# Attention bursts joined, cut with strips of several ordinary products, and TensorE's program aligned at six places, in a four-layer kernel on one core

## The chip, the core and the metric

The kernel runs on one of the eight cores of a Trainium2 chip. The metric is the time of one execution on the device in microseconds (us); lower is better. The core has engines that run side by side, each through its own list of instructions in order: TensorE (PE in the profile; its weight loads are PEld), VectorE (DVE), ScalarE (ACT), GpSimd (POOL) and SyncE (SP), which here issues nearly all DMAs. They wait for each other through semaphores.

## The reference

One sequence of 2048 positions with 448 features goes through two pairs of layers with the same weights in both pairs. Layer A is attention over 8 earlier positions at a distance of 2 (0, 2, ..., 14 back), with 16 heads of 28 features; layer B is a gated product.

```
def _A_ref(x, wqkv, wo):
    qkv = x @ wqkv                        # split in q, k, v; 16 heads of 28
    idx = pos[:, None] - (jnp.arange(8) * 2)[None, :]
    logits = einsum("bhsd,bhswd->bhsw", q, k[idx]) * 28 ** -0.5
    logits = where(idx >= 0, logits, -1e9)
    o = einsum("bhsw,bhswd->bhsd", softmax(logits), v[idx])
    return o.reshape(B, S, D) @ wo
def _B_ref(x, w_gate, w_up, w_down):
    return ((x @ w_gate) * (x @ w_up)) @ w_down      # 448 -> 1792 -> 448

x = x + _A_ref(layernorm(x), wqkv, wo)
x = x + _B_ref(layernorm(x), w_gate, w_up, w_down)
x = x + _A_ref(layernorm(x), wqkv, wo)
x = x + _B_ref(layernorm(x), w_gate, w_up, w_down)
```

## The kernel before

The layers are numbered 0 to 3 (A, B, A, B). The sequence is cut into chunks of 256 or 512 positions, and the chunks of the four layers are interleaved, so that layer 1 starts on the first chunk while layer 0 still works on later ones. `x_sb` holds the whole sequence on chip, all weights are loaded once.

**Ordinary products.** A product that sums over 448 features is cut into pieces of 64 rows. Two of them, on the two halves of TensorE's rows, run beside each other: the function `pair` makes one such step of two matmuls (recorded under L351). A unit is, for example, one block of 128 of the 1792 columns of layer B (`WGU`, 7 steps, 14 matmuls into two banks of PSUM), a pair of blocks of the down projection (`WD`), of the output projection (`wo_g`), of q and k (`WQK`) or of v (`WV`). `pair` also makes a second form of each step: 8 strips, each with 32 of the 128 columns of weights, on a tile of 64 x 32 of the array (L354). Eight strips do what the step's two matmuls do. A step whose end is signalled to another engine has no such form, and at most `MAXALT` = 6 steps of a unit have.

**Attention products.** Positions are worked on in blocks of 120 (the first of 128), two blocks a group, nine groups a layer. Here a group is named by layer and last block: S(0,10) is the scores of blocks 9 and 10 in layer 0. The scores "S" (L826) are keys times queries, in 64 small matmuls on tiles of 64 x 32; the groups named in `WIDE_S` take 32 matmuls on tiles of 64 x 64 in their place. ScalarE takes the exponential (L835), VectorE masks it with a minimum (L842). Then come 64 small matmuls "AV" (L860), the weighted sum of v together with the sum of weights, whose result is copied to `O_sb` (L871, L875), divided (L885 to L898) and goes into `oT`, the input of the output projection.

**Bursts.** The attention products use the array in another tiling than the ordinary ones, so they are issued as bursts. In the order of TensorE an entry `540*3.5/338` means: operation 540 (64 small products) is cut after 3 x 8 and 5 x 8 of them, at each cut one step of operation 338 is issued as its 8 strips, and what is left of 338 follows whole. An entry without `*` runs its small products one behind the other.

**What sets the order.** Nothing is decided at run time. `ORDER` has one string for each engine with the numbers of all operations in order; `BANKS` says which PSUM banks each operation of TensorE takes; both were written down by a search beforehand. `Sched.schedule` reads them, works out for each bank which operation must have released it, and `Sched.emit` issues the instructions with the waits on semaphores.

**Evictions.** Results leave PSUM by ScalarE or VectorE: q and k (`qk`, L701), v (`v_sb`, L766 to L793), gate by ScalarE to `g_sb` (L951), gate times up by VectorE to `hT` (L954), residuals by VectorE (L915). Layer norms take VectorE (L571, L573, L592) and ScalarE (L574, L576). The normed input is transposed by DMA (`dma_start_transpose`, SP) or, in layer 0, by TensorE (L602, L606).

Of the kernel before, what the change touches and what calls it, by code (L numbers as in the profile page):

```python
# [29 lines left out]
WIDE_S = ((0, 0), (0, 1), (0, 2), (0, 3), (0, 4), (0, 5))  # L30
MAXALT = 6
S_ORDER = (0, 4, 2, 6, 1, 5, 3, 7)
# [63 lines left out]
def grp_nc(g):  # L96
# [21 lines left out]
    ),  # L118
    "act": (
# [12 lines left out]
    ),  # L132
    "dve": (
# [18 lines left out]
    ),  # L152
    "pool": (
        "18 19 38 20 21 22 23 24 25 26 27 28 29 30 31 32 33 34 35 36 37"
# [45 lines left out]
class Sched:  # L200
# [22 lines left out]
    def schedule(self):  # L223
# [9 lines left out]
        for e in self.ENGS:  # L233
            self.order[e] = []
            for w in ORDER[e].split():
# [4 lines left out]
                if k:  # L240
                    short, cut, host = seq, [8 * int(c) for c in k.split(".")], self.ops[int(host)]
                    got.append(host)
                    k = len(cut)
                    cut += [len(short)]
                    seq, a = [], 0
                    for i, z in enumerate(cut):
                        seq += short[a:z]
                        a = z
                        if i < k:
                            seq += [(host, host.alt[i][q]) for q in (S_ORDER if short[z - 1][0].acquire.n == 4 else range(8))]  # L250
# [846 lines left out]
```

## Time and profile before

| | |
|---|---|
| median of 3 runs | 383.46 us (383.4, 383.46, 385.77) |
| profiled execution, first to last instruction | 380.8 us (the page gives no other time for it) |
| instructions profiled | 14251 |
| granted TensorE clock | 1.000 |
| DMA | 22.50 MB, mean 59 GB/s |

The profile is of one execution. It gives each engine's busy time, the chain of work that ended last, groups of instructions, waits with who ended them, and an order of time in which equal instructions are merged: start, length, engine, line, operation, output and inputs, shape, count. Matmuls are pipelined and their ends are modelled, so it is the starts of groups that tell how densely they follow. Shapes of matmuls are rows*columns of weights, then rows x moving columns.

### The profile page before, as it was taken

What the parts mean: (1) busy time and instruction counts of PE and PEld (TensorE: products, weight loads), DVE (VectorE), ACT (ScalarE), POOL (GpSimd) and SP (SyncE); (2) the same over time, 40 slices, a digit from 0 to 9 for tenths busy, and PEclk for the clock granted to TensorE, in tenths of its full rate; (3) what the DMA queues carried; (4) which work ended last, traced back from release to release, by engine and by line L of the source; (5) the groups of instructions that cost most, each with busy time, mean ns of one, the idle gap of its engine ahead of it and who ended that gap; (6) DMA issues with size and microseconds to landing.
All of it is one profiled execution on the core that took longest, in us unless ns stands there. A gap on an engine that the chain in (4) does not pass through costs nothing.

```text
span 380.8 us, 14251 instructions
## 1 busy us (share of the span) xinstructions
PE 375.8 (99%) x6322; PEld 210.2 (55%) x6322; DVE 287.0 (75%) x644; ACT 203.6 (53%) x389; POOL 5.1 (1%) x25
## 2 busy tenths in 40 slices
PE   8999999999999999999999999999999999999997
PEld 4645587545445445444756765545555444446664
DVE  8988999999976786787677985637998598455323
ACT  5997987746426652564465525547744635133320
POOL 5000000000000000000000000000000000000000
DMA  8656533600611034031101125320125004140002
GB/s 263 163 148 177 106 94 95 80 19 3 99 29 33 2 65 58 16 67 26 32 14 34 20 43 101 39 45 4 28 34 74 3 2 78 23 120 26 3 2 98
DMA packets 54881, 22.50 MB, mean 59 GB/s; under 512 B 45012, under 2 KB 54820, under 8 KB 54820
## 3 DMA queue, kind: packets, MB, share of 16 engines
q1 hardware_dynamic: 54676, 21.53, 27.6%
q8 instruction: 50, 0.82, 0.9%
q14 instruction: 11, 0.09, 0.1%
q10 hardware_dynamic: 144, 0.06, 0.1%
HBM read 8.54 MB, written 2.71 MB: 30 GB/s over the span
## 4 chain that ended last, share of the span: by engine, by line
PE 94%; DVE 2%; ACT 1%; issue 1%; DMA 1%; SPq 0%; DVEq 0%
PE ps L351 85%; PE ps L354 3%; PE ps L860 2%; PE ps L826 2%; PE ps L966 1%; ACT E_sb L835 1%; DMA x_sb<-in_A_x_dram 1%; DVE xn_sb L592 1%; DVE st L571 0%; PE ps L606 0%; DVE Qz L812 0%; DVE R_sb L885 0%; DVE E_sb L842 0%; SPq L443 0%; DVE qk L701 0%
## 5 line engine op out<-in xcount | busy, mean ns | idle before, releaser
L351 PE MATMUL ps<-xnTb,WGU 64*128 64x512 bf16 (+1 forms) x1894 | 172.4, 332 | 0.0
L351 PEld LDWEIGHTS ps<-xnTb,WGU 64*128 64x128 bf16 x1894 | 92.0, 94 | 69.8 <-issue 1.4
L951 ACT ACTIVATE g_sb<-ps 128x512 bf16<-128x512 f32 (+1 forms) x140 | 70.1, 510 | 85.0 <-PE ps L351 65.5
L954 DVE TENSOR_TENSOR hT<-g_sb,ps 128x512 bf16<-128x512 bf16 (+1 forms) x140 | 78.2, 575 | 46.9 <-ACT g_sb L951 44.4
L351 PE MATMUL ps<-WD,hT 64*128 64x448 bf16 x812 | 82.8, 350 | 0.0
L351 PEld LDWEIGHTS ps<-WD,hT 64*128 64x128 bf16 x812 | 38.9, 94 | 34.7 <-DVE hT L954 0.3
L351 PE MATMUL ps<-xnTa,WQK 64*128 64x512 bf16 (+1 forms) x494 | 53.0, 353 | 0.5 <-DVE WQK L518 0.3
L915 DVE TENSOR_TENSOR x_sb<-x_sb,ps 128x448 bf16<-128x448 bf16 x62 | 37.2, 614 | 14.7 <-PE ps L351 14.4
L835 ACT ACTIVATE E_sb<-ps,shift_sb 128x1024 bf16<-128x1024 f32 (+1 forms) x36 | 37.0, 1068 | 12.6 <-PE ps L826 12.4
L571 DVE BATCH_NORM_STATS2 st<-x_sb 128x6 f32<-128x448 bf16 x64 | 38.6, 616 | 1.3 <-DMA x_sb<-in_A_x_dram 0.8
L592 DVE TENSOR_SCALAR xn_sb<-x_sb,mv,rstd 128x512 bf16<-128x512 bf16 (+1 forms) x64 | 35.2, 566 | 5.5 <-ACT rstd L576 5.5
L701 ACT ACTIVATE qk<-ps 128x1024 bf16<-128x1024 f32 (+1 forms) x29 | 27.1, 947 | 15.6 <-PE ps L351 15.6
L351 PEld LDWEIGHTS ps<-xnTa,WQK 64*128 64x128 bf16 x494 | 23.0, 94 | 21.6 <-DVE WQK L518 0.5
L351 PE MATMUL ps<-wo_g,oT 64*128 64x448 bf16 x250 | 28.6, 350 | 0.0
L842 DVE TENSOR_TENSOR E_sb<-E_sb,MK 128x1024 bf16<-128x1024 bf16 (+1 forms) x36 | 23.4, 658 | 5.3 <-ACT E_sb L835 5.2
L886 ACT ACTIVATE R_sb<-R_sb 128x480 f32<-128x480 f32 (+1 forms) x34 | 20.2, 601 | 9.6 <-DVE R_sb L885 9.6
L898 DVE TENSOR_TENSOR oT<-O_sb,R_sb 128x480 bf16<-128x480 f32 (+3 forms) x36 | 22.1, 624 | 4.3 <-ACT R_sb L887 4.2
L351 PE MATMUL ps<-WV,xnTa 64*128 64x336 bf16 (+3 forms) x252 | 24.2, 305 | 0.1
L885 DVE STREAM_SHUFFLE R_sb<-O_sb 128x480 f32<-128x480 f32 (+1 forms) x34 | 23.1, 692 | 0.0
L574 ACT ACTIVATE lnv<-mv,eps_sb 128x2 f32<-128x2 f32 (+1 forms) x33 | 9.3, 291 | 22.2 <-DVE mv L573 22.2
L887 ACT ACTIVATE R_sb<-R_sb 128x480 f32<-128x480 f32 (+1 forms) x34 | 20.2, 601 | 0.5
L871 ACT ACTIVATE O_sb<-ps 128x512 f32<-128x512 f32 (+3 forms) x18 | 9.8, 557 | 14.9 <-PE ps L860 14.9
(60 smaller groups left out, 214.8 us busy)
## 6 DMA issues: line engine op xcount, KB each, us to landing
out_dram<-x_sb SPq DMA_DIRECT2D x15, 112.0 KB, 1.8
x_sb<-in_A_x_dram SPq DMA_DIRECT2D x3, 448.0 KB, 5.8
hT<-in_A_wqkv_dram SPq DMA_DIRECT2D x4, 224.0 KB, 4.4
WGU<-in_B_w_gate_dram SPq DMA_DIRECT2D x4, 224.0 KB, 3.9
WGU<-in_B_w_up_dram SPq DMA_DIRECT2D x4, 224.0 KB, 3.8
WD<-in_B_w_down_dram SPq DMA_DIRECT2D x2, 448.0 KB, 4.2
WGU<-in_B_w_gate_dram SPq DMA_DIRECT2D x2, 336.0 KB, 4.8
WGU<-in_B_w_up_dram SPq DMA_DIRECT2D x2, 336.0 KB, 4.4
```

The costliest lines, as they stand in the source:

```text
L351: return lambda E: E.matmul(out(), lhs(), rhs(), start=start, stop=stop)
L571: sc.add("dve", one(lambda E, B=B: E.bn_stats(st6[:, B, :], x_sb[:, B, :]), ("bn", li, B)), 525.0, deps=[("x", li - 1, B)] + ([("xn", li - ...
L592: sc.add("dve", one(lambda E, B=B, dst=dst, src=src: E.tensor_scalar(dst, src, mv[:, B, 0:1], rstd[:, B:B + 1], ALU.subtract, ALU.mult), ( ...
L701: return E.activation(dst, src, ACT.Copy) if hasattr(E, "activation") else E.tensor_copy(dst, src)
L835: return E.activation(E_sb[:, slot, 2 * hp:2 * hp + 2, 0:w], ps[:, b0:b0 + 2, 0:w], ACT.Exp, bias=shift_sb[:, 0:1], scale=SCALE)
L842: return E.tensor_tensor(e, e, MK[:, kind, 0:nc].unsqueeze(1).unsqueeze(1).to_broadcast([128, 2, w // nc, nc]), ALU.min)
L885: sc.add("dve", one(lambda E: E.stream_shuffle(R_sb[:, rs, 0:w], O_sb[:, os_, 0:w], [DH] * 32), ("Rs", li, qb)), dve_est(w) + 20.0, deps=[ ...
L886: sc.add("act", one(lambda E: E.activation(R_sb[:, rs, 0:w], R_sb[:, rs, 0:w], ACT.Ln), ("Rl", li, qb)), act_est(w, False), deps=[("Rs", l ...
L898: return E.tensor_tensor(oT[:, :, a % HALF:a % HALF + z - a], O[:, :, a - tok:z - tok], R_sb[:, rs, 0:w].rearrange("p (h n) -> p h n", h=4 ...
L915: sc.add("dve", one(lambda E: E.tensor_tensor(x_sb[:, B, :], x_sb[:, B, :], ps[:, bk[w], 0:D], ALU.add), ("x", li, B)), dve_est(D), deps=[ ...
L951: sc.add("act", one(lambda E, gs=gs, bk=bk: E.activation(g_sb[:, gs, 0:nt], ps[:, bk[0], 0:nt], ACT.Copy), ("G", li, j, fc)), act_est(nt), ...
L954: sc.add("dve", one(lambda E, gs=gs, bk=bk, fc=fc: E.tensor_tensor(hT[:, fc, hs, 0:nt], g_sb[:, gs, 0:nt], ps[:, bk[1], 0:nt], ALU.mult), ...
```

## The change

Three things change, all in TensorE's order and what reads it.

First, an entry of TensorE's order can join several bursts and take strips from several ordinary products. `596+613*1.2.3.4.6.7.8.9.11.12.13.14/484:6+485:6` issues the 64 products of AV(0,14) and the 64 of S(0,16) as one burst with twelve cuts; at the first six stand strips of operation 484, at the others strips of 485, and the whole matmuls left of both follow. Before, TensorE's order had 36 bursts (18 S, 18 AV), 18 of them without strips, and 55 runs of eight strips; after, it has 30 entries with bursts, six of them without strips, and 132 runs.

Second, an entry `~160` calls `addr_align(256, 160)`, which asks that the next instruction of TensorE's program stand at slot 160 of a block of 256 slots. There are six: ahead of AV(0,12), AV(2,2), S(2,6), S(2,12), AV(2,14) and AV(2,16), at slots 160, 168, 152, 16, 72 and 144.

Third, `WIDE_S` keeps only the first group, so five groups of layer 0 get 64 small score products in place of 32 larger ones; all orders and all banks are new, and 51 evictions change between ScalarE and VectorE. The operations themselves and their shapes are else the same. TensorE gets 6944 matmuls for 6322.

The diff, with the strings cut to what is spoken of:

```
-WIDE_S = ((0, 0), (0, 1), (0, 2), (0, 3), (0, 4), (0, 5))
+WIDE_S = ((0, 0),)
...
 ORDER = {
     "pe": (
-        "... 207 346 185 170 347 241 ... 263 348 ... 268 495 371 561 365 562 565 366 566 393 376 300 ..."
-        "... 540*3.5/338 339 523 580 ... 545*1.2.4.5/434 ... 596*1.2.4.5/654 ... 613*2.4.5/483 ..."
-        "... 1149*2.4.5/1072 ... 1132*2.4.5/1275 ... 1325*2.4.5/1232 ... 1308 1241 1330 ..."
+        "... 207 346 176 347 170 ... 241 ... 246+263 ... 268+371 490 ... 376*2.4.6/508:1+366:2 280 393 281 ..."
+        "... 540*1.2.4.5.6/339:5 ... 523*1.3.4.6/440:3+411:1 ... ~160 545*1.3.4.6/660:3+483:1 ..."
+        "... 596+613*1.2.3.4.6.7.8.9.11.12.13.14/484:6+485:6 ... 762+771*1.3.5.6.8.10/705:6 ..."
+        "... 1132+1149*1.2.3.4.6.7.8.9.11.12.13.14/1071:6+1072:6 ..."
+        "... 1308+1325*1.2.4.5.7.8.10.11.13.14/1234:4+1235:6 ... ~72 1330*1.2.3.4.5.6.7/1394:5+1298:2 ..."
...
@@ schedule
             for w in ORDER[e].split():
+                if w[0] == "~":
+                    self.order[e].append(([], [(None, int(w[1:]))]))
+                    continue
                 w, _, tail = w.partition("*")
-                k, _, host = tail.partition("/")
+                k, _, tail = tail.partition("/")
                 got = [self.ops[int(i)] for i in w.split("+")]
                 seq = [(o, n) for o in got for n in range(len(o.ins))]
                 if k:
-                    short, cut, host = seq, [8 * int(c) for c in k.split(".")], self.ops[int(host)]
-                    got.append(host)
-                    k = len(cut)
-                    cut += [len(short)]
+                    short, cut = seq, [8 * int(c) for c in k.split(".")] + [len(seq)]
+                    hosts = [(self.ops[int(i)], int(n)) for i, n in (h.split(":") for h in tail.split("+"))]
+                    strips = [(o, i) for o, n in hosts for i in range(n)]
+                    assert len(strips) == len(cut) - 1
+                    got += [o for o, _ in hosts]
                     seq, a = [], 0
                     for i, z in enumerate(cut):
                         seq += short[a:z]
                         a = z
-                        if i < k:
-                            seq += [(host, host.alt[i][q]) for q in (S_ORDER if short[z - 1][0].acquire.n == 4 else range(8))]
-                    seq += [(host, n) for n in range(2 * k, len(host.ins))]
+                        if i < len(strips):
+                            o, j = strips[i]
+                            seq += [(o, o.alt[j][q]) for q in (S_ORDER if short[z - 1][0].acquire.n == 4 else range(8))]
+                    seq += [(o, n) for o, m in hosts for n in range(2 * m, len(o.ins))]
...
@@ emit
                 for op, n in [x for _, seq in self.order[e] for x in seq]:
+                        if op is None:
+                            E.addr_align(256, n)
+                            continue
```

More of the change, by code (lines that the diff above doesn't have):

```diff
@@ L104 @@
     "pe": (
[13 rows of a table removed]
[16 rows of a table added]
     ),
     "act": (
[12 rows of a table removed]
[12 rows of a table added]
     ),
     "dve": (
[18 rows of a table removed]
[18 rows of a table added]
     ),
     "pool": (
-        "18 19 38 20 21 22 23 24 25 26 27 28 29 30 31 32 33 34 35 36 37"
+        "18 22 19 21 20 24 23 25 38 26 27 28 29 30 31 32 33 34 35 36 37"
     ),
     "sp": (
[5 rows of a table removed]
[5 rows of a table added]
     ),
@@ L285, in emit @@
             for got, seq in self.order[e]:
-                op = got[0]
-                if op.dma is not None:
+                op = got[0] if got else None
+                if op is not None and op.dma is not None:
                     sem = op.dma
@@ L292, in emit @@
                 for op, n in seq:
-                    if isinstance(n, int) and ((op.idx, n) in used or n == len(op.ins) - 1):
+                    if op is not None and isinstance(n, int) and ((op.idx, n) in used or n == len(op.ins) - 1):
                         count[e] += 1
```

129 rows, old and new, of tables (BANKS, ORDER) are left out of this document.

## The prediction

> **What bounds the kernel now.** I read the page's busy times and its chain first, then busy time by stage, then TensorE's order of time around the attention bursts.
>
> ```profile
> PE 375.8 (99%) x6322; PEld 210.2 (55%) x6322; DVE 287.0 (75%) x644; ACT 203.6 (53%) x389; POOL 5.1 (1%) x25
> PE 94%; DVE 2%; ACT 1%; issue 1%; DMA 1%; SPq 0%; DVEq 0%
> 0.00:65.00 65.00, 62.44 (x1206) 38.42 (x1207) 59.60 (x163) 53.92 (x105) 5.10 (x25) 1.00 0.58 149
> 65.00:381.00 316.00, 313.37 (x5122) 171.77 (x5116) 227.40 (x483) 149.71 (x285) 0.00 (x0) 1.00 0.23 40
> ```
>
> TensorE is the bound: 99% busy, 94% of the chain. In the two stages (length; PE, PEld, DVE, ACT, POOL busy) it idles 2.56 us of the first 65 and almost nothing after that but the end. So the time can only change through how densely TensorE's own products follow each other, or through a new wait. Only in the first 65 us is a second engine close: VectorE, 59.60 of 65.
>
> "Busy" hides what the change touches. How dense the stream is shows in the starts of its groups. First ordinary products (L351), which run in pairs:
>
> ```profile
> 131.91 4.70 PE L351 MATMUL ps<-xnTb,WGU 64*128 64x512 bf16 x42
> 136.44 0.59 PE L351 MATMUL ps<-WV,xnTa 64*128 64x336 bf16 x6
> ...
> 198.33 1.49 PE L351 MATMUL ps<-WD,hT 64*128 64x448 bf16 x14
> 199.75 0.68 PE L860 MATMUL ps<-E_sb,v_sb 64*32 64x64 bf16 x64
> 200.34 0.74 PE L826 MATMUL ps<-Qz,qk 64*32 64x64 bf16 x64
> 201.01 1.31 PE L351 MATMUL ps<-WD,hT 64*128 64x448 bf16 x12
> ```
>
> 21 pairs of 512 columns take 136.44 - 131.91 = 4.53 us, 0.216 a pair, so 448 columns take 0.189. Seven such pairs from 198.33 should end at 199.65; the burst of 64 attention products (L860, weights times V; "AV") starts at 199.75. **Entering a burst costs 0.10.** AV then takes 0.59, the 64 score products behind it (L826, "S") 0.67. A whole-product burst in this form therefore costs 0.69 to 0.71 for AV, 0.77 for S alone, and 1.36 for an AV and an S that follow each other.
>
> Now a burst with strips (L354, a quarter of a product's columns of weights each) of an ordinary product between the groups:
>
> ```profile
> 263.97 0.61 PE L351 MATMUL ps<-xnTa,WQK 64*128 64x512 bf16 x4
> 264.51 0.22 PE L860 MATMUL ps<-E_sb,v_sb 64*32 64x64 bf16 x8
> 264.55 0.40 PE L354 MATMUL ps<-xnTb,WGU 64*32 64x512 bf16 x8
> 264.77 0.21 PE L860 MATMUL ps<-E_sb,v_sb 64*32 64x64 bf16 x8
> 264.80 0.40 PE L354 MATMUL ps<-xnTb,WGU 64*32 64x512 bf16 x8
> 265.01 0.24 PE L860 MATMUL ps<-E_sb,v_sb 64*32 64x64 bf16 x16
> 265.07 0.40 PE L354 MATMUL ps<-xnTb,WGU 64*32 64x512 bf16 x8
> ...
> 265.53 0.27 PE L860 MATMUL ps<-E_sb,v_sb 64*32 64x64 bf16 x24
> 265.74 0.82 PE L351 MATMUL ps<-xnTb,WGU 64*128 64x512 bf16 x6
> 266.40 0.73 PE L351 MATMUL ps<-wo_g,oT 64*128 64x448 bf16 x6
> ```
>
> Each run of eight strips takes 0.22 (264.55 to 264.77), the same as the pair it replaces; eight attention products between two strips take 0.03, sixteen 0.06: 3.6 ns each against 9.2 (0.59/64) in the plain burst. The strips give the sequencer time to run ahead. The last 24 take 0.21, of which 24 x 3.6 = 0.09 is work: **leaving costs 0.12**. From 264.51 to 266.40 are 1.89; the host's seven pairs are 1.51; with 0.10 for entering, a stripped AV costs 0.48.
>
> ```profile
> 151.31 0.22 PE L826 MATMUL ps<-Qz,qk 64*32 64x64 bf16 x8
> ...
> 153.24 0.54 PE L351 MATMUL ps<-WD,hT 64*128 64x448 bf16 x4
> ...
> 22.14 1.03 PE L351 MATMUL ps<-xnTa,WQK 64*128 64x512 bf16 x8
> 23.09 0.64 PE L826 MATMUL ps<-Qz,qk 64*64 64x128 bf16 x32
> 23.67 0.82 PE L351 MATMUL ps<-xnTa,WQK 64*128 64x512 bf16 x6
> ```
>
> A stripped S: 1.93 - 1.51 + 0.10 = 0.52. The wide S (32 products of 64 x 64, no strips): 0.58 + 0.10 = 0.68.
>
> **The change, part by part: bursts.** I count bursts from the two orders; S(0,0), AV(0,0) and all columns of ordinary products stay as they are. Before: wide S, 5 x 0.68 = 3.40; plain AV alone, 6 x 0.70 = 4.20, and one more right behind an S, 0.60; the adjacent pair AV(2,4), S(2,6), 1.36; the two half-size bursts of layer 2, 0.44 and 0.40 (estimates: half of 0.67 and of 0.59, with 0.10); stripped S, 9 x 0.52 = 4.68, and one with a single strip, 0.65 (estimate, between 0.52 and 0.77); stripped AV, 7 x 0.48 = 3.36, and one that follows a burst, 0.38. Sum 19.5.
>
> After: S(0,2) and S(0,8) are narrow and plain, 2 x 0.77 = 1.54; AV(0,2)+S(0,4) and AV(0,4)+S(0,6) are joined without strips, 2 x 1.36 = 2.72; eleven stripped AV, 5.28; eight stripped S, 4.16; the half-size S, 0.44; three joined AV+S with strips, each 0.48 + 0.52 less one entry and one exit (0.22), 3 x 0.78 = 2.34; the half-size AV joined with a stripped S, 0.52 + 32 x 0.0036 = 0.64. Sum 17.1. **Bursts: -2.4 us.** Bounds: -3.0, if the shorter last groups (16 or 8 instead of 24) save their 0.03 too; -1.6, if the 77 added runs of strips cost 0.01 each over the pairs they replace, the last place of the rows.
>
> The added strips buy little where a burst had four already; the gain sits in the eight plain AV and in the three joins. The wide S given up cost 0.09 each where they stay plain, two places. TensorE gets 6944 products for 6322: 160 more S, 616 more strips, 154 fewer ordinary ones.
>
> ```profile
> L860 PE MATMUL ps<-E_sb,v_sb 64*32 64x64 bf16 x1024 | 14.2, 193 | 0.0
> ```
>
> 1024 AV products cover 14.2 us in all, strips between them included. [...]
>
> **The fill at the six aligned places.** Each asks that the next instruction stand at a given slot of 256, so slots ahead of it are filled. Counting two slots a product and one a wait, 98, 21, 105, 45 and 125 slots are filled at the second to sixth place; at the first anything from 0 to 255, since its absolute place is not known. The sequencer passes them in its turn and the engine sees them only when its stock runs out. No row shows a fill. Bounds:
>
> ```profile
> L328 PEldq EVENT_SEMAPHORE  x134: 51/51/1127, 1.4 to 370.7; - x134
> L328 ACTq EVENT_SEMAPHORE  x66: 17/17/17, 7.9 to 366.9; - x66
> q8 instruction: 50, 0.82, 0.9%
> ```
>
> From below 4.6 ns a slot (9.2 for the two slots of a plain AV product), from above 51, TensorE's wait; the same wait on ScalarE is 17. A fill waits for nothing, so I take 17. What covers it: a strip run lets the sequencer store at least 16 products, as the groups of sixteen at 3.6 ns show, and 24 in the last group; 24 stored ordinary products last 12 x 0.216 = 2.6 us. At 17 ns 125 slots take 2.1, so five places cost nothing and the first at most 255 x 0.017 - 2.6 = 1.7. I take 0; a fill that gains time is excluded, since it does no work. Without the cover (51 ns): 98, 105 and 125 slots cost 2.4, 2.8 and 3.8, and the first 0 to 10.4.
>
> The program is fetched in 50 packets (0.82 MB: 16 KB, 256 slots); 0.9% of 16 engines over 380.8 us is 55 us, 1.1 us a packet. A plain joined burst uses 256 slots in 1.26, so if anything waits there it is for 0.3 or less, twice. I take 0 for what the alignment gains: no burst of before shows a wait of this kind.
>
> **The order and the banks.** Waits of TensorE that the new order moves lie in the first 65 us:
>
> ```profile
> 20.92 0.82 PE L351 MATMUL ps<-xnTa,WQK 64*128 64x512 bf16 x6 [0.32 <-DVE WQK L518]
> 22.01 0.29 PE L606 MATMUL ps<-ident,xn_sb 64*128 64x64 bf16 x8 [0.15 <-ACT E_sb L835]
> 44.18 0.50 PE L351 MATMUL ps<-xnTa,WQK 64*128 64x256 bf16 x6 [0.21 <-DVE O_sb L875]
> 47.42 0.64 PE L826 MATMUL ps<-Qz,qk 64*64 64x128 bf16 x32 [0.45 <-DVE qk L701]
> ...
> PE ps L502 <- DVE hT L473: 1.3, 1, 1.3
> ```
>
> The first stays: the same product follows the same burst. S(0,8), which waited 0.45, now comes behind AV(0,6) with its strips. The one at 22.01 gets a product ahead of it. New is S(0,6) inside a burst: its banks are freed by the eviction of the product right ahead of that burst, with AV's 0.59 between; up to 0.3. Behind it in TensorE's order stand the next QK products, and ScalarE's exponentials wait for it. Net -0.5; bounds -1.0, when all but the first vanish, and +1.0, if a new one stands for each. 51 evictions change between ScalarE and VectorE, 26 to VectorE and 25 from it; that moves about one us in 287. The DMA queue's issues keep their order up to 30 us or so; behind that, transposes were nowhere waited for by TensorE, so I leave them at 0.
>
> **Sum:** -2.4 + 0 - 0.5 = -2.9. The profiled span is 380.8 and becomes 377.9. The page gives no time for that execution beside its span; the median of the runs, 383.46, stands 2.7 above, start and end of the program, which stay. So 380.6.
>
> **Rivals.**
> 1. *The fill is not hidden* (slower). Place: the sequencer ahead of AV(0,12), AV(2,2), S(2,6), S(2,12), AV(2,14), AV(2,16). At TensorE's wait price, 51 ns, 9.0 us at three places and 0 to 10.4 at the first, say 4: 380.6 + 9 to 13, about 391. It decides from 2.6/125 = 21 ns a slot up. For: the 51 of the row is of the same sequencer. Against: that instruction tests a semaphore. Chance 0.20.
> 2. *VectorE becomes the bound of the first 65 us.* It has 5.4 us of slack there; by the prices above the bursts of that stage get cheaper by 0.4, the waits by 0.5. If VectorE holds the stage at its length and TensorE waits once more for 0.5 at each of three evictions, 380.6 + 0.9 + 1.5 = 383.0: nothing gained. For: 59.60 of 65. Against: most of its waits in front of TensorE had slack. Chance 0.15.
> 3. *The new order also takes out what idles in the first stage.* 2.56 us idle there, 1.3 of it ahead of the first product (the last row above); with the rest gone, and the bursts at their -3.0, 380.6 - 0.8 - 0.6 = 379.2. Chance 0.15.
>
> **How the numbers follow.** The forecast has 0.50, its own range 378.9 to 382.5. About 1% is what a measurement can tell from no change: 379.6 and 387.3. Faster by more: rival 3 mostly (0.12) and two fifths of the forecast's spread (0.20), 0.32. Slower: rival 1 nearly whole and a tail of rival 2, 0.23. The rest, 0.45, within. The range runs from 377.6 (rival 3 with half a us more) to 391, which leaves out the worse half of rival 1 and little below.
>
> **What would show it.** Right: PE's busy time and chain share as before, span near 378; stripped AV at 0.48 and joined AV+S at 0.78 over their hosts; no idle at the six places. The bursts are wrong if a run of strips takes over 0.23 or groups of sixteen over 0.08. Rival 1: TensorE idles for 2 us or more just ahead of the aligned bursts, named as issue or its sequencer. Rival 2: waits on VectorE's evictions before 65 us in PE's list. A wait inside a joined burst, between its AV and its S, would show the join wrong.

## The result and the profile after

The changed kernel takes 423.39 us (median of 4, 420.65 to 424.09) against 383.43 for the kernel before: a ratio of 1.100, interval 1.0939 to 1.106. The forecast was 380.6, its range ended at 391. The profiled execution took 423.21 us, span 421.4.

The page of the changed kernel: busy times, the granted clock in 40 slices, the queue that fetches instructions, and the chain that ended last.

```profile
PE 386.6 (92%) x6944; PEld 219.7 (52%) x6944; DVE 291.2 (69%) x645; ACT 203.6 (48%) x388; POOL 5.0 (1%) x25
PEclk9999989999959999979999999999989999599999
q8 instruction: 57, 0.93, 0.9%
PE 87%; issue 6%; DVE 5%; DMA 1%; ACT 1%; DVEq 0%
```

Two things are new. TensorE idles 34.8 us of the span (it was 5.0), and although its bursts were made shorter it is busy 10.8 us longer, with slices at half clock. TensorE's waits name the idle time (us in total, times, longest):

```profile
PE ps L871 <- issue: 19.8, 3, 7.4
PE ps L837 <- issue: 5.6, 1, 5.6
PE ps L362 <- DMA xnTb<-xn_sb: 2.6, 1, 2.6
PE ps L871 <- DVE Qz L823: 1.3, 1, 1.3
```

The first, second and fourth lines are AV and S bursts (L871, L837) at five of the six aligned places, 26.7 us together. The fourth is the place with 45 slots. It names a Qz of VectorE, but an AV reads only E_sb and v_sb: the Qz ended at 326.03 us, the last NOP was issued at 325.89 and the burst starts at 326.06, 0.18 behind that NOP, as at the second place. The fill itself appears as NOP of TensorE's sequencer, in the view of its line: all of them, then the 128 of the first place, each with duration and first and last start.

```profile
L324 PEldq NOP  x522: 13/13/13, 110.8 to 362.9; - x174
L324 PEldq NOP  x128: 13/13/13, 110.8 to 120.1; - x128
```

TensorE's timeline at that place:

```profile
110.16 2.81 PE L362 MATMUL ps<-WD,hT 64*128 64x448 bf16 x28
120.40 0.26 PE L871 MATMUL ps<-E_sb,v_sb 64*32 64x64 bf16 x8 [7.42 <-issue]
```

Busy time by stretch behind it and 10 us later (columns: length, PE, PEld, DVE, ACT, POOL, then the granted clock):

```profile
121.00:125.00 4.00, 4.00 (x100) 1.95 (x85) 1.35 (x3) 1.01 (x2) 0.00 (x0) 0.50 0.02 4
130.00:134.00 4.00, 4.00 (x144) 2.22 (x141) 2.82 (x5) 1.80 (x4) 0.00 (x0) 1.00 0.18 37
```

Each NOP is recorded with 13 ns, but 128 of them take 110.8 to 120.1: **73 ns each**. The products that TensorE still has in stock cover the first 2.0 of those 9.3 us, then it idles 7.42. And when it starts again, at 120.40 us, it runs at half clock (0.50) until 126.05. 522 NOPs were counted in advance rightly (98, 21, 105, 45, 125 behind the unknown first, which is 128); what one costs was not.

### The profile page after: what moved, and what is told of

Same layout as the page of the kernel before. It is cut to its first block, busy times and chain, and to the rows that moved or that the text cites. A ratio compares the mean times of both kernels' runs of the same rounds, so it can differ in the third digit from the quotient of the medians.

```text
span 421.4 us, 16077 instructions
## 1 busy us (share of the span) xinstructions
PE 386.6 (92%) x6944; PEld 219.7 (52%) x6944; DVE 291.2 (69%) x645; ACT 203.6 (48%) x388; POOL 5.0 (1%) x25
## 4 chain that ended last, share of the span: by engine, by line
PE 87%; issue 6%; DVE 5%; DMA 1%; ACT 1%; DVEq 0%
PE ps L362 73%; PE ps L365 7%; PE ps L837 2%; PE ps L871 2%; PE ps L513 2%; PE ps L977 1%; DMA xnTb<-xn_sb 1%; DVE x_sb L926 1%; DVE xn_sb L603 1%; DVE hT L965 0%; DVE oT L909 0%; DVE Qz L823 0%; DVE st L582 0%; DVE E_sb L853 0%; PE ps L617 0%
## 5 line engine op out<-in xcount | busy, mean ns | idle before, releaser
L362 PE MATMUL ps<-xnTb,WGU 64*128 64x512 bf16 (+1 forms) x1916 | 182.3, 337 | 2.7 <-DMA xnTb<-xn_sb 2.6
L362 PEld LDWEIGHTS ps<-xnTb,WGU 64*128 64x128 bf16 x1916 | 96.1, 95 | 75.8 <-issue 6.6
L362 PE MATMUL ps<-WD,hT 64*128 64x448 bf16 x664 | 72.7, 359 | 0.3 <-ACT g_sb L962 0.3
L362 PEld LDWEIGHTS ps<-WD,hT 64*128 64x128 bf16 x664 | 32.8, 96 | 30.2 <-issue 4.5
L871 PE MATMUL ps<-E_sb,v_sb 64*32 64x64 bf16 (+1 forms) x1088 | 22.5, 201 | 21.3 <-issue 19.8
L882 ACT ACTIVATE O_sb<-ps 128x512 f32<-128x512 f32 (+3 forms) x23 | 12.1, 547 | 42.0 <-PE ps L871 42.0
L871 PEld LDWEIGHTS ps<-E_sb,v_sb 64*32 64x32 bf16 x1088 | 16.5, 96 | 29.9 <-issue 23.5
L837 PE MATMUL ps<-Qz,qk 64*32 64x80 bf16 (+2 forms) x1072 | 21.5, 199 | 5.8 <-issue 5.6
L882 DVE COPY O_sb<-ps 128x448 f32<-128x448 f32 (+2 forms) x13 | 8.2, 633 | 26.8 <-PE ps L871 26.8
L365 PE MATMUL ps<-WD,hT 64*32 64x448 bf16 x704 | 25.4, 375 | 0.7 <-issue 0.7
```

What stands on the lines that cost most here:

```text
L362: return lambda E: E.matmul(out(), lhs(), rhs(), start=start, stop=stop)
L365: return lambda E: E.matmul(out()[c:c + 32], lhs()[:, c:c + 32], rhs(), start=start, stop=stop, tile_position=(row, c))
L837: ins.append((lambda E, hc=hc, c=c, s_=s_, p=p, b=b, h=h, ks=ks, qs=qs, lo=lo, hi=hi: E.matmul(ps[64 * c + KN * s_:64 * c + KN * s_ + KN, ...
L871: ins.append((lambda E, b=b, c=c, o=o, vw=vw, eb=eb, eo=eo: E.matmul(ps[32 * b:32 * b + 32, bk[c], o:o + nc], vw, E_sb[64 * c:64 * c + 64, ...
```

## The experiments

Theory A: the executed fill makes the loss, 73 ns a slot beyond the cover (the work that TensorE still has in stock), and the half clock after it. Rivals: B, the joins and the new orders lose by themselves; C, the positions matter. Later D: what is left is SyncE's order; E: the orders only fit together.

**The fill alone, on the kernel before.** The same counts ahead of the same bursts, nothing else changed (one place shown):

```
- 452 536 545*1.2.4.5/434 464 ...
+ 452 536 ~5 545*1.2.4.5/434 464 ...        # 128 slots; likewise 98, 21, 105, 45, 125
```

> The kernel before with the same fill alone: 128, 98, 21, 105, 45 and 125 filling instructions ahead of the same six bursts (O+S products 545, 776, 938, 1303, 1330 and 1352), all orders, bursts and banks as before. Theory A (the fill by itself makes the loss): about 27 us of idle and about 9.6 us of half clock, 383.4 + 37 = 420 us, within 414 to 426. Rival B (the joins and new orders lose): under 390 us. The prediction's price (17 ns a slot, 2.6 us of cover) gives 383.4 to 384 us, its upper end (51 ns) 392 to 400 us.

Measured 422.88 us, ratio 1.101 (1.0953 to 1.1068): a loss as large as the change's, without one join. The busy times of its page:

```profile
PE 386.6 (92%) x6322; PEld 212.8 (50%) x6322; DVE 288.0 (68%) x644; ACT 204.1 (48%) x389; POOL 5.1 (1%) x25
```

TensorE's waits in it:

```profile
PE ps L866 <- issue: 21.5, 3, 7.3
PE ps L832 <- issue: 5.4, 1, 5.4
PE ps L866 <- DVE R_sb L891: 2.3, 1, 2.3
PE ps L832 <- DVE O_sb L881: 1.4, 1, 1.4
```

The clock behind its first place:

```profile
95.00:99.00 4.00, 4.00 (x100) 1.86 (x86) 2.09 (x8) 1.19 (x2) 0.00 (x0) 0.50 0.02 4
```

The span grew by 422.1 - 380.8 = 41.3. The four waits are 30.6. The same 6322 products are busy 386.6 us against 375.8: 10.8 more, the half clock. 30.6 + 10.8 = 41.4. Nothing is left for another cause here. (That the total agrees with the changed kernel's within 0.5 us is chance, as the branch below shows: there the fill costs 34.0 us, not 39.5. On the kernel before, two of the six places stand right behind a burst and one behind seven pairs that follow a burst, where less is covered: 30.6 us of waits against 26.7.)

**A ladder of fills on the kernel before**, 16, 24, 32, 48, 64 and 96 slots ahead of the same six bursts (the same edit with other slots).

> The kernel before with 16, 24, 32, 48, 64 and 96 filling instructions ahead of the same six bursts, to read the price and the cover from a ladder. Theory A (72 ns each, some 1.8 us of cover by work already queued on TensorE): idle of 0, 0, 0.5, 1.7, 2.8 and 5.1 us, about 10 us, and a fall of the granted clock only behind the last or the last two, 1.5 to 5 us more: 393 to 399 us. Rival (51 ns each and 2.6 us of cover, the upper end of the prediction): 0, 0, 0, 0, 0.7 and 2.3 us, 386.4 us. Price of 17 ns: 383.4 us.

Measured 401.87 us, ratio 1.0481 (1.0411 to 1.0552): more than expected. Behind 16 slots there is no wait. TensorE's timeline at the other five, with what stood ahead and the wait of the burst in brackets:

```profile
163.94 0.34 PE L866 MATMUL ps<-E_sb,v_sb 64*32 64x72 bf16 x32
166.01 0.22 PE L866 MATMUL ps<-E_sb,v_sb 64*32 64x64 bf16 x8 [1.73 <-DVE xn_sb L598]
...
202.28 0.68 PE L866 MATMUL ps<-E_sb,v_sb 64*32 64x64 bf16 x64
205.34 0.68 PE L832 MATMUL ps<-Qz,qk 64*32 64x64 bf16 x64 [2.38 <-DVE R_sb L891]
...
273.87 3.19 PE L357 MATMUL ps<-xnTb,WGU 64*128 64x512 bf16 x28
278.24 0.22 PE L832 MATMUL ps<-Qz,qk 64*32 64x64 bf16 x8 [1.18 <-DVE oT L904]
...
290.98 1.50 PE L357 MATMUL ps<-WD,hT 64*128 64x448 bf16 x14
296.14 0.68 PE L866 MATMUL ps<-E_sb,v_sb 64*32 64x64 bf16 x64 [3.67 <-issue]
...
328.39 0.26 PE L866 MATMUL ps<-E_sb,v_sb 64*32 64x64 bf16 x8 [4.82 <-issue]
```

Behind the 48 the clock stays at 1.00 (278 to 281 us). Behind the 64:

```profile
296.50:299.50 3.00, 3.00 (x50) 1.49 (x46) 0.35 (x1) 2.57 (x5) 0.00 (x0) 0.54 0.03 5
```

At 73 ns the fills last 1.8, 2.3, 3.5, 4.7 and 7.0 us. Take off the waits: the cover is 2.3 and 2.2 us behind long ordinary products (48 and 96 slots), 1.0 behind seven pairs that follow a burst (64), and **nothing behind a burst** (24 and 32). So the price was as Theory A had it and the cover was not one number.

**No aligned place, and a branch over the fill.** Two edits of the changed kernel:

```
- ... 654 478 479 ~160 545*1.3.4.6/660:3+483:1 ...
+ ... 654 478 479 545*1.3.4.6/660:3+483:1 ...      # all six out

- E.addr_align(256, n)
+ E.addr_align(256, n, 0)                          # no NOP executed: a branch over the padding
```

> The changed kernel with its six aligned places taken out and nothing else: the joins, the strips and all orders stay. Theory A (the fill costs): the trace of the changed kernel shows 522 fill instructions 71 to 74 ns apart, about 27.4 us of idle TensorE behind them and about 9.6 us lost to the half clock after that idle, so 423.2 - 37.0 = 386.2 us, within 383 to 388; what is left above 383.4 is the 3.0 us wait for a transposing transfer at 51 us and the 1.7 us of half clock behind it. Rival B (the joins and the new orders themselves lose): above 400 us. Rival C (the aligned places are needed, as the change has it): stops for instruction fetches appear in several joined bursts, some 1.1 us each as at 216.9 us of the changed kernel, and the time is 388 to 392 us.

> The changed kernel with its six aligned places reached by a branch over the filling instead of through it: same orders, same positions in the 256-slot blocks, no fill executed. Theory A (each executed fill instruction costs some 72 ns, the position nothing): 384 to 392 us, that is the 386.2 us expected without the aligned places plus six branches of 0 to 1 us each. Rival C (the positions are what costs or gains): if positions gained, this would lie below the kernel without the aligned places by 1 us or more; if positions cost, it stays above 400 us. No NOP should be left in TensorE's queue, and the granted clock should not fall behind the six places.

Measured 391.93 (ratio 1.0203, 1.0109 to 1.0297) and 389.39 us (1.0136, 1.0082 to 1.019). Of the 40 us, 34.0 go when the fill is not executed. The first lies above Theory A's 383 to 388 and inside Rival C's range. The second lies inside its 384 to 392 and 2.5 below the first, which is Rival C's mark. Both are still 6 us and more above the kernel before, so the new orders lose something too: less than B had it, but a part. In the kernel with the branch, the view of the aligning line:

```profile
L324 PEldq COMPARE_BRANCH  x6: 170/185/295, 112.2 to 330.5; - x6
```

TensorE's timeline where the first branch stands:

```profile
111.79 2.62 PE L362 MATMUL ps<-WD,hT 64*128 64x448 bf16 x26
114.34 0.22 PE L871 MATMUL ps<-E_sb,v_sb 64*32 64x64 bf16 x8
```

Thirteen pairs of 448 take 2.46, and the burst starts 2.55 after the first: entry 0.09, so a branch of 0.17 to 0.30 us is covered whole. At the other five places the entry is 0.09 too. TensorE's waits of over 1 us in it, the first product's left out:

```profile
PE ps L362 <- DMA xnTb<-xn_sb: 2.8, 1, 2.8
PE ps L362 <- issue: 2.1, 1, 2.1
PE ps L837 <- issue: 1.5, 1, 1.5
PE ps L365 <- issue: 1.1, 1, 1.1
```

and one issue of SyncE's queue:

```profile
66.20 0.40 SPq L454 DMA_DIRECT2D WD<-in_B_w_down_dram  x1
```

The first wait is for transposes; the second ends at 69.6, as the last part of WD, issued at 66.20, lands (WD's loads took 3.2 to 4.8). The third and fourth are stops in joined burst AV(2,12)+S(2,14) and in burst AV(2,4), at ends of 256-slot blocks (slots 0 and 254, counted from the aligned place before them).

**SyncE's queue, by hand.** On the kernel with the branch:

```
- ... 359 358 368 369 510 293 291 504 91 505 503 501 500 ... 515 88 578 583 90 429 ...
+ ... 359 358 293 291 368 369 510 504 91 88 505 503 501 90 500 ... 515 578 583 429 ...
```

> The kernel that branches over its fill, with four issues in SyncE's queue moved ahead: the two transposes into xnTb (291, 293) ahead of the three into v_sb (368, 369, 510), and the weight loads WD (88, 90) ahead of copies into vt and transposes. Nothing moves on the other engines. Theory: the 2.8 us at 51 us and the 2.3 us at 67 us, with the half clock that follows them in the profiled run (1.7 us), are made by SyncE's order alone: 389.4 - 5.1 - 1.7 = 382.6 us, 382 to 384.5. Rival: something else is late at the same places (VectorE, which is the busiest engine there), and the time stays above 386 us.

Measured 391.3 us (1.0219, 1.015 to 1.0289): a miss. Both waits were gone and one of 6.5 us stood at 71.7:

```profile
PE ps L362 <- DMA xnTb<-xn_sb: 6.5, 1, 6.5
```

SyncE's queue ahead of it:

```profile
60.02 3.34 SPq L721 DMA_DIRECT2D vt<-qk  x9
63.40 4.49 SPq L732 DMA_TRANSPOSE v_sb<-vt  x3
...
69.61 1.30 SPq L606 DMA_TRANSPOSE xnTb<-xn_sb  x1
...
72.50 3.98 SPq L606 DMA_TRANSPOSE xnTb<-xn_sb  x3
```

The next four transposes into xnTb stand behind these nine copies and three transposes into v_sb. So the queue was late as a whole, and the first two waits had only been its first signs. The next edit moves these four ahead as well. Three transposes into v_sb (511, 516, 515) come ahead of six copies with them, and the load 90 goes three places back:

```
- 501 90 500 502 506 573 574 577 575 576 579 511 516 515 578 583 429 584 427 431 433 589
+ 501 500 502 506 90 429 511 427 433 431 516 515 573 574 577 575 576 579 578 583 584 589
```

> As the kernel with the branch and four of SyncE's issues moved (391.3 us), whose trace had TensorE wait 6.5 us at 71.7 us for transposes into xnTb that stood in SyncE's queue behind nine copies into vt and four transposes into v_sb: here 429, 427, 433 and 431 are moved ahead of these as well. Theory D: the wait shrinks to 0 to 1 us and the half clock behind it (6.8 us at half speed, about 3 us) goes: 391.3 - 6 - 3 = 382 us, 380.5 to 385. Rival E: another wait takes its place and the time stays above 387 us.

**381.82 us, ratio 0.9971 (0.9945 to 0.9997)**: Theory D. TensorE's program is that of the changed kernel, but for the branch. Busy times and chain of its page:

```profile
PE 374.5 (99%) x6944; PEld 215.4 (57%) x6944; DVE 289.6 (76%) x645; ACT 202.8 (53%) x388; POOL 5.0 (1%) x25
PE 98%; ACT 1%; issue 1%; DVE 0%
```

Its only waits over 0.2 us:

```profile
PE ps L513 <- DVE qmask L508: 1.2, 1, 1.2
PE ps L365 <- issue: 1.0, 1, 1.0
```

The moved transposes in SyncE's queue:

```profile
59.72 1.97 SPq L606 DMA_TRANSPOSE xnTb<-xn_sb  x1
63.81 4.80 SPq L606 DMA_TRANSPOSE xnTb<-xn_sb  x3
```

Putting SyncE back to the order of the kernel before, instead, is no cure:

> The kernel that branches over its fill, with SyncE's queue alone put back to the order of the kernel before; TensorE, VectorE, ScalarE and the positions are those of the change. Theory D (what is left of the loss, 389.4 - 383.4 = 6 us, is made by SyncE's new order: transposes and weight loads queued behind copies and other transposes): 381 to 385 us, with no wait of over 1 us for xnTb or WD before 90 us. Rival E (the new orders of the computing engines need the new SyncE order, and the old one makes other waits): 386 us or more, with waits at other tiles, v_sb above all.

409.12 us (1.0667, 1.0641 to 1.0693): E held, though at another tile than it named. TensorE waits 12.0 us for transposes into xnTb at four places and only 1.6 for v_sb. SyncE's order of before doesn't fit the new orders of the other engines.

**What positions are worth.** With SyncE's queue mended by the first four moves, and no aligned place:

> As the kernel with SyncE's four issues moved, but with no aligned place at all. It tells what alignment is worth once it costs nothing. By the run of the changed kernel without aligned places, which had stops of 1.5, 0.9 and 2.2 us at block boundaries in dense stretches against 1.4 and 1.7 us with them: 0.5 to 2.5 us slower than the same kernel with the six places branched to, 383 to 386.5 us. If position is worth nothing: the same time.

395.96 us (1.031, 1.026 to 1.0359) against 391.3 beside it: 4.7 us slower, where 0.5 to 2.5 were forecast. On the 381.8 us kernel:

> The 381.8 us kernel without any aligned place: what the six positions are worth when nothing is paid for them and SyncE's order does not stand in the way. By the two pairs measured so far (391.9 against 389.4, and 396.0 against 391.3): 2 to 5 us slower, 384 to 387 us, with stops at block boundaries inside joined bursts 596+613 and 1308+1325 as in those runs. If position is worth nothing, as the prediction had it: 381 to 382.5 us.

386.17 us (1.0075, 1.0049 to 1.0101): 4.4 more. With the first pair (391.93 and 389.39) the position is worth 2.5 to 4.7 us; the 2.5 lies within the spread of that pair's slower kernel (388.4 to 394.1). Much of it goes into stops: in the profiles those named issue, without the wait for WD, make 2.6, 0.1 and 1.2 us with the six places and 3.6, 4.0 and 3.6 without. TensorE's timeline of the 386.17 us kernel shows the longest of its stops, inside joined burst AV(2,12)+S(2,14):

```profile
289.56 0.35 PE L365 MATMUL ps<-WD,hT 64*32 64x448 bf16 x1
291.43 0.37 PE L365 MATMUL ps<-WD,hT 64*32 64x448 bf16 x5 [1.52 <-issue]
```

That is the matmul at which a 256-slot block ends (slot 254). The queue that fetches instructions tells the rest: its packet that began at 288.97 had landed at 289.98, 1.45 us before the matmul. All stops at block ends of 0.6 us and more in these runs end 1.2 to 1.6 us behind the landing of a packet of that queue. So C held too, in the change's favour. An attempt to find better positions failed:

```
- 921*1.2.3.4.5.6/860:5+855:1 861 856 ~152 938*...       ~16 1303*2.4.6/...
+ ~8 921*1.2.3.4.5.6/860:5+855:1 861 856 938*...         ~54 1303*2.4.6/...
```

> As the kernel with the branch and SyncE's four issues moved, and two of the six aligned places changed: the one ahead of 938 goes ahead of burst 921 (slot 8), and the one ahead of 1303 goes from slot 16 to 54, so that the 256-slot boundary falls in the middle of joined burst 1308+1325. Theory (fetch stops of 1.4 us in burst 921 and 1.7 us in 1308+1325 are a matter of where the boundary falls): 1.0 to 3.0 us under the run beside it with the old places, 380.5 us, 379.5 to 382.5, and both stops gone from the trace. Rival (a burst of this density stops somewhere whatever its place): the same time as the run beside it, with the stops at other matmuls.

396.11 us (1.031, 1.0263 to 1.0356) against 391.3. TensorE idles 1.5 and 1.7 us at block ends in the joined bursts at 1132 and 1308 and 0.7 at the moved place at slot 8, while the run beside it, with the old places, has no such stop over 0.2. My rule for a safe place, a boundary in the middle of a burst, was wrong. And one strip fewer in burst 921, on the 381.8 us kernel:

```
- 921*1.2.3.4.5.6/860:5+855:1 861
+ 921*1.2.3.4.5/860:5 855 861
```

> The 381.8 us kernel (branch over the fill, SyncE's order mended) with one strip fewer in burst 921, so that product 855 follows it whole. In that kernel's trace TensorE stops 1.3 us in this burst, at the matmul where a 256-slot block ends, with the last strip; with five strips the block ends seven wide matmuls behind the burst. Theory (the stop is a late instruction fetch and needs a dense stretch up to the boundary): 381.8 - 1.3 = 380.5 us, 379.8 to 381.3, and under the kernel before by 0.5 to 0.9%. Rival (the fetch is late for another reason, such as the transfers beside it): 381.5 to 382.5 us, with the stop at the same boundary or another.

382.07 us, ratio 0.9963 (0.9941 to 0.9985), with a stop of 1.3 us in the same burst. I had placed the boundary behind the burst; it lies inside (slot 254), so the run doesn't test the theory. It repeats that the order, free of its fill, is 0.4% ahead of the kernel before.

**The bursts alone, on the order before:**

```
- 762 776*1.2.4.5/827 ...        921 938 855 ...              1330 1297 1242 ...
+ 762+776*2.4.5.7.8.10/827:6 ... 921+938*1.3.5.9.11.13/855:6  1330*1.2.4.5/1297:2+1242:2 ...
```

> The kernel before, with its own orders, banks and S tiles, in which only bursts are changed: the plain bursts 212, 246, 268, 376, 398, 523, 757, 1308 and 1330 get strips of the products that follow them, and 762+776 and 921+938 are joined with strips. No aligned place. By the prediction's prices (0.22 us for an AV burst that gets strips, 0.25 for an S burst, 0.22 for a join) seven bursts of 64, two of 32 (half as much), two joins: 383.4 - 2.7 = 380.7 us if every step pays, 380 to 382.5. If the joins and strips are worth nothing or cost a wait for banks or fetches: 383 to 386 us. A stop within a burst at a boundary of 256 slots, some 1 to 2 us, would show the fetch as the new limit.

388.17 us (1.0103, 1.0067 to 1.0139): slower. TensorE at burst 1330:

```profile
289.25 0.22 PE L868 MATMUL ps<-E_sb,v_sb 64*32 64x64 bf16 x8
290.41 0.34 PE L362 MATMUL ps<-WV,xnTa 64*32 64x336 bf16 x8 [0.94 <-DVE O_sb L883]
```

The strips bring product 1297 forward, and its banks are not yet free. TensorE's list has nine such new waits of 0.1 to 0.9 us, 3.0 of the 4.0 us by which the span grew. Where none stands the burst got cheaper as priced (1308 by 0.23, 921 and 938 by 0.23 and 0.19). A strip is a use of its host's banks and inputs at an earlier time. The change gives the strips a new order and new banks, and in the 381.8 us kernel no such wait is over 0.2 us.

## Why the prediction was wrong, step by step

**The step that failed is the price of the fill**: "A fill waits for nothing, so I take 17." It is 73 ns, outside even the bounds taken from the rows of semaphore waits (4.6 to 51). An instruction of another kind is no bound for one that no row shows, and with hundreds of them on the engine that bounds the kernel, the price decided everything. The range was cut too short as well: at its own upper price and with the longest first fill the prediction's terms give 380.6 + 9.0 + 10.4 = 400 us, and the range ended at 391. Rival 1 named the place and the sign ("decides from 21 ns"), and its mark, idle time ahead of the aligned bursts named as issue, is what the trace shows. It was sized at 9 to 13 us; by 73 ns less a cover of 2.2 its places give 7.1, 5.0, 0, 5.5, 1.1 and 6.9, 25.6 of the 26.7 seen.

**Its second term was missing**: the clock. TensorE never idled over 1.3 us in the profile before and kept the full clock (1.000), so no row told of it. In the fill alone it made 10.8 of 41.3 us.

**The cover** of 2.6 us was near (1.9 to 2.3) behind long products, and wrong behind a burst.

**Alignment at 0** was wrong by 2.5 to 4.7 us. "0.3 or less, twice" came from the fetch's 1.1 us against a burst's 1.26 us; the stops are 1.0 to 2.0. That no burst of before waited was no evidence: its blocks of 256 slots lasted 2.7 us or more, while the densest after the change last 1.8.

**Transposes at 0** was wrong: 389.39 - 381.82 = 7.6 us hung on SyncE's order, which I had followed only up to 30 us.

**The bursts** were nearly right. In the 381.8 us kernel a stripped AV costs 0.46 to 0.52 over its hosts (once 0.57), a stripped S 0.51 or 0.52; 0.48 and 0.52 were forecast. The joined burst AV(2,12)+S(2,14) on TensorE's timeline there:

```profile
286.36 0.22 PE L871 MATMUL ps<-E_sb,v_sb 64*32 64x64 bf16 x8
...
289.68 1.67 PE L362 MATMUL ps<-xnTb,WGU 64*128 64x512 bf16 x14
```

3.32, less 14 pairs of its hosts at 0.189, 2.65, with 0.10 for entering: 0.77; 0.78 was forecast. The two others cost 0.93 and 1.00, so the price of a join held in one of three. Summed in the same way over all groups, with 0.10 for each entry, bursts fall from 21.1 to 18.8 us, once the one stop of 1.34 is taken off: -2.3, forecast -2.4.

**The waits** of the new order came near too: TensorE's idle times of over 0.1 us, stops at block ends left out, fall from 2.5 to 1.8 us, -0.7 where -0.5 was forecast. The span fell by 0.8; bursts, waits and the stops (-2.3 - 0.7 + 1.5) make -1.5, and the 0.7 between them isn't assigned.

**Rival 2** did not come: TensorE's waits for VectorE stayed at 1 to 2 us. **Rival 3**'s time, 379.2, was not reached either.

From median to median the change is thus: new order and bursts without positions, with SyncE's mended queue, 383.4 to 386.2 (+2.8, stops at block ends among it); positions, -4.4; SyncE's order, +7.6; executed fill, +34.0; 423.4 together. The stages were taken away in one sequence only, so another sequence may share the time out differently, and the first of them mixes orders, bursts and banks.

**What stays open:** why one stop in burst 921 persists, and at which block ends TensorE stops. The same program of TensorE stopped at different places from run to run, and in the 381.8 us kernel three blocks that lasted only 1.8 to 1.9 us ended without a stop, so a dense block alone doesn't make one.

## What to carry to other kernels

The padding that aligned code was executed here: on the engine that bounds the kernel it cost its count times the price of a NOP (73 ns, beyond a cover of 0 to 2.3 us), and behind its long idle times the half clock cost again (10.8 us in the fill alone); a branch over it was free at the change's six places (entry 0.09 us at each). Before an operation that no row shows is priced, ask what the time is at ten times the guess, and carry that into the range. An order searched for one engine is only as good as the in-order queues that feed it: read the DMA queue's order to the end of the stage that it feeds.

## What the runs showed of the hardware

- A NOP of TensorE's sequencer: 13 ns in its record, 73 from start to start (128 of them from 110.8 to 120.1 us in the changed kernel). By place the mean over the 522 is 73 to 77 ns. In the ladder the waits behind 48 and 96 slots, 1.18 and 4.82 us, differ by 76 ns a slot.
- The granted clock was 0.50 in five stretches of the changed kernel's trace: 54.37 to 57.78 us, 115.81 to 126.05, 184.07 to 190.90, 310.37 to 313.78 and 358.15 to 368.39. They last 3.41, 10.24, 6.83, 3.41 and 10.24 us, and the first two begin 61.44 us apart, 18 times 3.413. In the 3.41 us right ahead of them TensorE idles 2.61, 2.84, 3.41, 3.41 and 2.11 us. In steps of 3.41 us counted on from the first, the most that it idles in a step with full clock in it and in the next is 1.66 (303.54 to 306.95). Four stretches of 3.41 us of the kernel with the branch (length, PE busy, and the granted clock, third from the end): the idle 2.83 us at 51.39 are spread over two, 1.24 and 1.60, and the clock stays at 1.00; the idle 2.08 at 67.56 stand in one, and the next is at 0.50. What idle time the clock bears beyond these values was not shown.

```profile
49.21:52.62 3.41, 2.17 (x78) 0.97 (x74) 3.37 (x10) 3.41 (x5) 0.00 (x0) 1.00 0.85 154
52.62:56.03 3.41, 1.81 (x34) 1.84 (x36) 1.62 (x3) 0.96 (x4) 0.00 (x0) 1.00 0.67 143
66.28:69.69 3.41, 1.33 (x24) 0.89 (x22) 3.40 (x8) 0.86 (x4) 0.00 (x0) 1.00 0.72 169
69.69:73.10 3.41, 3.41 (x46) 1.44 (x54) 0.82 (x3) 0.60 (x1) 0.00 (x0) 0.50 0.99 102
```

- Queue q8, of kind instruction, moved 50 packets of 16 KB before and 57 after. TensorE's recorded instructions in the two traces (products, weight loads, waits, NOPs), 12782 and 14568, make 49.9 and 56.9 times 256.
- In bursts with strips TensorE stopped for 1.0 us (the 381.8 us kernel) to 2.0 us (the 396.0 us kernel) at ends of 256-slot blocks, each stop of 0.6 us and more ended 1.2 to 1.6 us behind the landing of a packet of q8. In the changed kernel it issued the last product of such a block at 216.93 us and the next at 218.03, 1.49 behind the landing of a packet that took from 215.34 to 216.54.
- Of the six branches, of 0.17 to 0.30 us, five stay in their block and one goes into the next; at all six the entry into the burst is 0.09 us, against 0.10 in the kernel before. The place that was moved to slot 8 is reached by a branch into the next block too, and TensorE idles 0.7 us there; why was not shown.
